# Joined exponentials over a double PSUM tile, and a unit's outputs copied in two halves, in a fused attention and MLP block

## The chip, the cores and the metric

The kernel runs on one core of a Trainium2 chip. The metric is the device time in microseconds (us), the median over runs. The engines of a core are named as the profile names them: PE does matmuls (PEld is its loading of weights), ACT is ScalarE, DVE is VectorE, POOL is GpSimd, and SP issues most of the DMAs. Matmul results land in PSUM, eight banks of 512 fp32 values in each of 128 partitions; ACT and DVE read them from there.

## The reference

All arrays are fp32. One sequence of 2048 tokens with width 512 goes through a layer norm; the result feeds a self-attention with 32 heads of width 16 and an MLP whose output is a gate.

```
def _A_ref(x, wqkv, wo):
    qkv = (x @ wqkv).reshape(B, S, 3, H, Dh) -> q, k, v        # H = 32, Dh = 16
    scores = einsum("bhqd,bhkd->bhqk", q, k) * (Dh ** -0.5)
    p = softmax(scores, axis=-1)
    o = einsum("bhqk,bhkd->bhqd", p, v)
    return o.reshape(B, S, D) @ wo
def _B_ref(x, w1, b1, w2, b2):
    return gelu(x @ w1 + b1) @ w2 + b2                          # 512 -> 1376 -> 512
xn = layernorm(x)
return x + _A_ref(xn, ...) * silu(_B_ref(xn, ...))
```

## The kernel before

The kernel has two parts. The first computes the layer norm, the projections and the MLP, with every product split in high and low parts for precision. The second is the attention. It also ends with the output projection.

**Units and steps.** Heads are taken in 8 groups of 4, queries in 4 chunks of 512. One group and one chunk make a *unit*, so there are 32 units. A unit has 16 *steps*, one for each block of 128 keys, 512 steps in all. In step n (unit `ua`, block `ka` = n mod 16) PE computes for each of the four heads the transposed scores of the block, 128 keys by 512 queries, into one PSUM bank (a *T*, function `t_one`). ACT takes the exponential of each (`slot<-pst` or `slot<-ps` in the profile). PE then multiplies the exponentials of the step *before* with the values, for four heads into one bank `pv` (a *V*, `pv_step`), which sums over the unit's 16 steps. The value matrix carries a column of ones, so that row 16 of each head's 32 output rows is the softmax denominator.

**Maxima.** Before a unit can be exponentiated, the maximum of every row of its scores is needed. This is a second pass over the scores with queries as rows: matmuls of 128 queries by 512 keys (line 183), each followed by a maximum on DVE (line 189). There are 2048 of them. The first part places 576 between its own matmuls (`fill`); the steps of the attention place three each, until they are used up after about 491 steps. In a step two of the three are whole (*S*); the third is made of two halves, *X* and *Y*, of 256 columns each, which share a bank and are reduced together once Y is there. The banks of these matmuls go round in a ring of three (`s_ring`). When a unit's 64 maxima are there, `s_end0` reduces them on DVE (line 242), transposes them (line 246, once for two units as long as the unit is below `PAIRED`), POOL splits them in high and low parts, and `s_send` writes them to DRAM some steps later (`later`, `tick`, `flush`); `load_mh` reads them back as two extra rows of the unit's queries, so that T subtracts them. `need` is the step at which that load is placed.

**Row halves.** T and S use 50 and 48 rows of the array, either the lower 64 rows (`a` = 0) or the upper (`a` = 1). Two matmuls on different halves run side by side. In the first part the matmuls of the projections stand in pairs, one on each half, and `fill(a)` puts a maximum's matmul on one half at a time.

**The order of a step** is written by hand as a string: `ORDER[3]`, with other strings for `ka` 0 and 2 (`AFTER`), and `ORDER[0]` for the last steps, which have no maxima left. There the output projection of the first tokens (`w_halves`) runs instead. `todo` hangs loads, moves and divisions on single T of a step.

**PSUM for T.** Four banks go round: `ps_m` for the first T of a step, the three of `ps_t` for the others.

**End of a unit.** After the sixteenth V, DVE copies the 128 by 512 outputs to the SBUF tile `os` (line 779); only for the last unit ACT copies one half and DVE the other (lines 781, 782). `o_move` sends the denominators and the four heads' rows out of `os` by five DMAs; `o_den` takes reciprocals and spreads them through DRAM (`den_d`, `dn`); `o_div` divides on POOL. `os` is one buffer, and `pv` one bank, so the next unit's first V waits for the copy.

Of the kernel before, what the change touches and what calls it, by code (L numbers as in the profile page):

```python
# [8 lines left out]
F32 = mybir.dt.float32  # L9
# [31 lines left out]
ORDER = {0: "TTTTV", 3: "TSXTTSTYV"}  # L41
AFTER = {0: "STXTTSTYV", 2: "XTSTTYSTV"}
HC = CH // 2
PAIRED = 28
# [6 lines left out]
def fused(ctx: ExitStack, tc: tile.TileContext, x, wqk, wv, wo, w1, b1, w2, b2, out):  # L51
# [7 lines left out]
    ps_t = ctx.enter_context(tc.tile_pool(name="ps_t", bufs=3, space=PSUM))  # L59
    ps_v = ctx.enter_context(tc.tile_pool(name="ps_v", bufs=1, space=PSUM))  # L60
    ps_m = ctx.enter_context(tc.tile_pool(name="ps_m", bufs=1, space=PSUM))

# [4 lines left out]
    den_d = dpool.tile([NG * NCH, GH, CH], F32, name="den_d")  # L67
# [98 lines left out]
    def flush():  # L166
        while later and later[0][0] <= 0:
            u = later.pop(0)[1]
            run_off()
            s_send(u)  # L170
# [36 lines left out]
    def s_op(op):  # L207
# [6 lines left out]
        elif op == "X":  # L214
# [5 lines left out]
            run_off()  # L220
# [11 lines left out]
    def run_off():  # L232
        while put_off:
            put_off.pop(0)()

    def s_end0(u):
# [6 lines left out]
        if u == us[-1]:  # L243
            later.append([12 if "seen" in prog else 8, us[0]])
            nt = qring.tile([P, 2 * GH * NCH], F32, name="nt")
            nc.vector.transpose(nt, nm)
            mh = MH[us[0]] = qring.tile([P, 2, 2 * GH * NCH], F32R, name="mh")

        def two():
            if u == us[-1]:  # L250
                nc.gpsimd.tensor_copy(mh[:, 0], nt)
                nc.gpsimd.tensor_sub(mh[:, 1], nt, mh[:, 0].bitcast(F32))

        put_off.append(two)
        if "seen" in prog or u == NU - 1:
            run_off()
# [128 lines left out]
    with ExitStack() as s1:  # L385
# [4 lines left out]
        def a_tile(shape):  # L390
# [4 lines left out]
            return ps_t.tile(list(shape), F32, name="pst")  # L395
# [220 lines left out]
    def down(c, f, part):  # L616
        i = c * FT + f
        if f == 0 and part == 0:
            PA[c] = [ps_v.tile([P, D], F32, name="pv")] + [ps_t.tile([P, D], F32, name="pst") for t in range(3)]
# [49 lines left out]
    def quad(n, at):  # L669
        us = first[n]  # L670
        for u, b in zip(us, BANKS[n]) if at == 0 else ():
            pool, name = {"x": (ps_x, "ps"), "m": (ps_m, "ps"), "v": (ps_v, "pv"), "t": (ps_t, "pst")}[b]
# [16 lines left out]
    turns, PN = [0], []  # L689

    def t_tile():
        turns[0] += 1
        if turns[0] < 5:
            pool = (ps_m, ps_x, ps_a, ps_b)[turns[0] - 1]
        else:
            pool = ps_m if turns[0] % 4 == 1 else ps_t
        return pool.tile([P, CH], F32, name="pst" if pool is ps_t else "ps")

    def t_one(u, k, p, a):
# [4 lines left out]
        ps = t_tile()  # L704
# [341 lines left out]
```

## Time and profile before

| what | us |
|---|---|
| median of 3 runs | 1563.26 (1563.18 to 1563.92) |
| profiled execution, its own time | 1564.16 |
| span of the profiled execution | 1562.4 |
| PE busy | 1555.6 |
| DVE busy | 1414.8 |
| ACT busy | 1232.5 |
| POOL busy | 366.8 |

All views are of that one execution. The attention takes about the last 1090 us of the span. Three engines are nearly full there, so busy shares alone do not tell which of them sets the pace: one has to look at which wait ends last within a step. A matmul's length in the rows is modelled; its start is not. A row with `x3` is three instructions that followed each other, with the time from the first one's start to the last one's end. Instructions overlap: an exponential's row is 0.60 us long, but the next one starts 0.48 us after it.

### The profile page before, as it was taken

The page shows a single profiled execution, that of the slowest core. Times are in us where ns is not written, and L with a number is a line of the kernel's source. Part 1 is how long each engine was busy: PE and PEld are TensorE (multiplying, and loading weights), DVE is VectorE, ACT ScalarE, POOL GpSimd, SP SyncE. Part 2 cuts the span into 40 slices and gives each one's busy share as a digit, 9 for nine tenths or more (in the row PEclk, how much of TensorE's full clock was granted, in tenths as well). Part 3 has the DMA queues.
Part 4 walks back from the last instruction along what each step waited for, and adds up shares of the span by engine and source line. Part 5 has one row for each costly group of instructions (what it writes and reads, how often), then busy time and mean ns, then how long its engine had stood idle before and what let it go on. Part 6 is the DMA issues. An engine that isn't in the chain of part 4 may idle for free.

```text
span 1562.4 us, 31826 instructions
## 1 busy us (share of the span) xinstructions
PE 1555.6 (100%) x12246; PEld 955.1 (61%) x12246; DVE 1414.8 (91%) x2294; ACT 1232.5 (79%) x2393; POOL 366.8 (23%) x367
## 2 busy tenths in 40 slices
PE   9999999999999999999999999999999999999999
PEld 8899999999994444444444444444444444444455
DVE  7599999999989999999999999999999999999834
ACT  4333332434349999999999999999999999999984
POOL 4145675756650011001000100100010000000143
PEclk9999999999999999999999999999999999999999
DMA  6625343454322123114201411411151111110163
GB/s 209 153 60 152 122 139 100 156 146 136 116 97 62 38 43 59 29 39 63 67 25 27 70 43 30 70 33 29 28 79 26 33 29 33 40 30 22 46 198 114
DMA packets 78584, 116.88 MB, mean 75 GB/s; under 512 B 27972, under 2 KB 28228, under 8 KB 77256
## 3 DMA queue, kind: packets, MB, share of 16 engines
q1 hardware_dynamic: 74684, 101.89, 23.6%
q0 software_dynamic: 3264, 12.35, 4.7%
q8 instruction: 97, 1.59, 0.4%
q14 instruction: 55, 0.45, 0.1%
q10 hardware_dynamic: 484, 0.60, 0.1%
HBM read 84.35 MB, written 25.97 MB: 71 GB/s over the span
## 4 chain that ended last, share of the span: by engine, by line
PE 97%; DVE 1%; DMA 1%; ACT 0%; issue 0%; DVEq 0%
PE pv L772 33%; PE pst L706 14%; PE ps L580 13%; PE ps L706 12%; PE ps L183 12%; PE pst L580 7%; PE pv L580 2%; PE ps L896 1%; PE ps L452 1%; PE ps L81 1%; PE pst L81 0%; DVE st L411 0%; DMA dn<-den_d 0%; DMA xt<-in_x 0%; PE pst L434 0%; DMA dr<-os 0%
## 5 line engine op out<-in xcount | busy, mean ns | idle before, releaser
L189 DVE TENSOR_REDUCE mx<-ps 128x2 f32<-128x512 f32 x2048 | 1316.2, 686 | 83.7 <-PE ps L183 43.1
L708 ACT ACTIVATE slot<-pst 128x512 f32<-128x512 f32 x1533 | 803.9, 606 | 0.6 <-PE ps L706 0.6
L772 PE MATMUL pv<-slot,vsb 128*32 128x512 f32 x4096 | 545.3, 605 | 0.5 <-DVE os L779 0.5
L183 PE MATMUL ps<-kt,slot 48*128 48x512 f32 (+1 forms) x1364 | 378.3, 368 | 0.0
L708 ACT ACTIVATE slot<-ps 128x512 f32<-128x512 f32 x515 | 307.5, 598 | 13.7 <-PE ps L706 6.2
L706 PE MATMUL pst<-qt,kt 50*128 50x512 f32 x1149 | 307.0, 403 | 0.4 <-DVE gt L639 0.3
L183 PEld LDWEIGHTS ps<-kt,slot 48*128 48x128 f32 x1364 | 225.6, 184 | 41.9 <-DVE mx L189 37.3
L706 PEld LDWEIGHTS ps<-qt,kt 50*128 50x128 f32 x387 | 70.6, 183 | 282.7 <-ACT slot L708 281.7
L580 PE MATMUL ps<-slot,w1h 64*128 64x512 f32 x1088 | 226.0, 392 | 0.0
L706 PEld LDWEIGHTS pst<-qt,kt 50*128 50x128 f32 x1149 | 208.1, 185 | 19.3 <-DVE gt L639 1.0
L183 PE MATMUL ps<-kt,qz 48*128 48x512 f32 x512 | 202.6, 396 | 0.0
L706 PE MATMUL ps<-qt,kt 50*128 50x512 f32 x387 | 190.8, 495 | 0.0
L183 PE MATMUL ps<-slot,slot 48*128 48x512 f32 (+1 forms) x598 | 165.8, 367 | 0.0
L580 PEld LDWEIGHTS ps<-slot,w1h 64*128 64x128 f32 x1088 | 155.8, 185 | 7.9
L580 PE MATMUL ps<-slot,w1l 64*128 64x512 f32 x544 | 159.5, 392 | 0.0
L772 PEld LDWEIGHTS pv<-slot,vsb 128*32 128x32 f32 x4096 | 80.7, 108 | 100.0 <-issue 91.1
L364 ACT ACTIVATE hg<-ps,b_sb 128x512 f32<-128x512 f32 x44 | 27.9, 685 | 134.0 <-PE ps L580 122.6
L371 POOL TENSOR_TENSOR hl<-hg,hh 128x512 fp32r<-128x512 f32 x76 | 96.8, 1296 | 153.2 <-ACT hh L370 119.7
L183 PEld LDWEIGHTS ps<-slot,slot 48*128 48x128 f32 x598 | 98.6, 184 | 17.0 <-DVE mx L189 15.3
L706 PE MATMUL pst<-qt,slot 50*128 50x512 f32 x384 | 100.5, 404 | 0.0
L183 PEld LDWEIGHTS ps<-kt,qz 48*128 48x128 f32 x512 | 93.7, 183 | 0.8 <-DVE mx L189 0.5
L810 POOL TENSOR_TENSOR ot<-ot,dn 64x512 f32<-64x512 f32 x15 | 19.2, 1280 | 301.1 <-DMA dn<-den_d 257.6
(159 smaller groups left out, 1718.0 us busy)
## 6 DMA issues: line engine op xcount, KB each, us to landing
raw<-in_w SPq DMA_DIRECT2D x88, 256.0 KB
qk_h<-hh SPq DMA_DIRECT2D x32, 256.0 KB
qk_l<-hl SPq DMA_DIRECT2D x32, 256.0 KB
qt<-qk_h SPq DMA_DIRECT2D x128, 64.0 KB
slot<-qk_h SPq DMA_DIRECT2D x92, 64.0 KB
g_d<-gt POOLq DMA_DIRECT2D x16, 256.0 KB, 3.5
qt<-qk_l SPq DMA_DIRECT2D x64, 64.0 KB
dn<-den_d SPq DMA_DIRECT2D x32, 128.0 KB
```

The lines of the kernel that those rows point to most:

```text
L81: nc.tensor.matmul(ps, lhs[a], rhs[b], start=first and n == 0, stop=last and n == 2)
L183: return nc.tensor.matmul(ps[:, c0:c0 + w], QS[u][r, p, qi * P:(qi + 1) * P], kts[u // NCH % KB][p][r, k0:k0 + w], start=True, stop=True).ins
L189: nc.vector.tensor_reduce(MX[u][:, 2 * p:2 * p + 2, qi, ki][:, heads, parts], ps.rearrange("p (n c) -> p n c", c=HC), axis=AX.X, op=OP.max)
L364: nc.scalar.activation(raw, ph.pop(u), AF.Gelu_apprx_tanh, bias=b1_sb[:, u[2]:u[2] + 1])
L371: nc.gpsimd.tensor_sub(hl, raw, hh.bitcast(F32))
L452: nc.tensor.matmul(pq["q", g, c], W1[g][i][:, k * P:(k + 1) * P], (xh, xl)[j][c][:, k], start=n == 0 and k == 0, stop=n == 2 and k == KT - 1)
L580: i = nc.tensor.matmul(ps, lhs[r], rhs[r], start=first, stop=last).ins
L706: nc.tensor.matmul(ps, kts[g % KB][p][r, k * P:(k + 1) * P], QT[u][r, p, :], start=True, stop=True)
L708: nc.scalar.activation(PT[u, k][:, 2 * p + a, :], ps, AF.Exp, scale=SCALE)
L772: nc.tensor.matmul(PV[u][32 * j:32 * j + 32, :], vsb[:, k, h:h + 32], PT[u, k][:, j, :], start=(k == 0), stop=(k == NT - 1))
L810: eng.tensor_mul(ot[c][rs, g // 2], ot[c][rs, g // 2], DN.pop(u)[rs])
L896: HALF[0] = nc.tensor.matmul(PW[i][0], OTS[i, k][x][r], (wo_h, wo_l)[y][r, k], start=k == 0 and side == 0 and n == 0, stop=k == KT - 1 and ...
```

## The change

- The PSUM pool `ps_t` (three banks) becomes `spare` in the first part, and is closed at the first attention step. In its place come a pool of one bank (`ps_t`) and a tile `two` of two banks, made once.
- `SIDES` gives the four T of a step as (pair of heads, row half). The first goes to `ps_t`, the second and third to the two banks of `two`, the fourth to `ps_m`. The two in `two` are heads 0 and 1 of the group, one on each row half; one exponential of 1024 elements takes both. So a step has three exponentials.
- All steps with three maxima have the order `XTSTTYSTV`; `AFTER` is gone.
- Every unit's outputs are copied by ACT (first 256 columns) and DVE (the others) into two tiles. `o_move` takes 10 DMAs, `o_den` spreads the denominators with 2 instead of 1, and `den_d` has the halves as a dimension.
- `s_end0` leaves the transpose and POOL's two operations to `s_turn`, which runs a step later; in the step with `ka` = 1 neither is done. The sending comes 12 ticks later instead of 8, `need` grows by one or two steps, and `PAIRED` is 26 instead of 28.

```
-ORDER = {0: "TTTTV", 3: "TSXTTSTYV"}
-AFTER = {0: "STXTTSTYV", 2: "XTSTTYSTV"}
+ORDER = {0: "TTTTV", 3: "XTSTTYSTV"}
+SIDES = ((1, 1), (0, 0), (0, 1), (1, 0))
-PAIRED = 28
+PAIRED = 26
...
+    def s_turn(u, nm):
+        later.append([8 if u == NU - 1 else 12, u])
+        nt = qring.tile([P, 2 * GH * NCH], F32, name="nt")
+        nc.vector.transpose(nt, nm)
+        mh = MH[u] = qring.tile([P, 2, 2 * GH * NCH], F32R, name="mh")
+        nc.gpsimd.tensor_copy(mh[:, 0], nt)
+        nc.gpsimd.tensor_sub(mh[:, 1], nt, mh[:, 0].bitcast(F32))
...
+    def t_bank(i):
+        return TP["one"].tile([P, CH], F32, name="pst") if i == 0 else TP["two"][:, i - 1]
+    def t_one(u, k, i, pair=False):
+        p, a = SIDES[i]
...
+        if u == k == 0:
+            ps = (ps_m, ps_x, ps_a, ps_b)[i].tile([P, CH], F32, name="ps")
+        elif i == 3:
+            ps = ps_m.tile([P, CH], F32, name="ps")
+        else:
+            ps = t_bank(i)
...
-        nc.scalar.activation(PT[u, k][:, 2 * p + a, :], ps, AF.Exp, scale=SCALE)
+        if not pair or i in (0, 3):
+            nc.scalar.activation(PT[u, k][:, 2 * p + a, :], ps, AF.Exp, scale=SCALE)
+        elif i == 2:
+            nc.scalar.activation(PT[u, k][:, :2], TP["two"], AF.Exp, scale=SCALE)
...
+    sp.close()
+    TP["one"] = ctx.enter_context(tc.tile_pool(name="ps_t", bufs=1, space=PSUM))
+    TP["two"] = ctx.enter_context(tc.tile_pool(name="ps_2", bufs=1, space=PSUM)).tile([P, 2, CH], F32, name="two")
...
-            OS[u] = wb.tile([P, CH], F32, name="os", bufs=1)
+            OS[u] = [wb.tile([P, HC], F32, name=f"os{i}", bufs=1) for i in range(2)]
             pv = PV.pop(u)
-            if u < NU - 1:
-                nc.vector.tensor_copy(OS[u], pv)
-            else:
-                nc.scalar.activation(OS[u][:, :HC], pv[:, :HC], AF.Copy)
-                nc.vector.tensor_copy(OS[u][:, HC:], pv[:, HC:])
+            nc.scalar.activation(OS[u][0], pv[:, :HC], AF.Copy)
+            nc.vector.tensor_copy(OS[u][1], pv[:, HC:])
...
+        for i in range(2):
+            engs[i].dma_start(DR[u][64 * i:64 * i + 64], os[i][DH::32])
...
-            need = min(n for n in range(L) if due(n) >= 64 * (units_of(u)[-1] + 1)) + (9 if u < PAIRED else 4 if u < NU - 1 else 2)
+            last = units_of(u)[-1]
+            need = min(n for n in range(L) if due(n) >= 64 * (last + 1))
+            need += 10 if u < PAIRED else 6 if u < NU - 1 else 2
...
+        if ka == 1:
+            pass
+        elif put_off:
+            s_turn(*put_off.pop(0))
+        else:
+            for u in list(ended):
+                if u >= PAIRED or ka > 2 and since.setdefault(u, n) < n:
+                    s_end0(u)
```

The order of the instructions shows three places. First PE in an inner step, before (T is L706, S and the 256-column X and Y are L183, V is L772; `kt` are keys, `qt` and `slot_4443` queries, the other slots exponentials):

```order
L706 MATMUL ps<-qt_614,kt_609 128x512
L183 MATMUL ps<-kt_609,slot_4443 128x512
L183 MATMUL ps<-kt_609,slot_4443 128x256
L706 MATMUL pst<-qt_614,kt_609 128x512 x2
L183 MATMUL ps<-kt_609,slot_4443 128x512
L706 MATMUL pst<-qt_614,kt_609 128x512
L183 MATMUL ps<-kt_609,slot_4443 128x256
L772 MATMUL pv<-slot_18503,vsb 32x512 x4
```

and now (T is L703, V is L775):

```order
L183 MATMUL ps<-kt_609,slot_4443 128x256
L703 MATMUL pst<-qt_6826,kt_609 128x512
L183 MATMUL ps<-kt_110,slot_4443 128x512
L703 MATMUL two<-qt_6826,kt_609 128x512 x2
L183 MATMUL ps<-kt_609,slot_4443 128x256
L183 MATMUL ps<-kt_110,slot_4443 128x512
L703 MATMUL ps<-qt_6826,kt_609 128x512
L775 MATMUL pv<-slot_17979,vsb 32x512 x4
```

X has moved to the front, ahead of the first T and the first S; the second S stands behind Y, and the last T is the step's last matmul before V. The second T of the pair follows the first in the program, on the other row half.

Second, ACT in the attention, before, where a change of units leaves no mark on it (a `slot` takes the four exponentials of one step):

```order
L708 ACTIVATE slot_12819<-ps 128x512 [waits PE_49]
L708 ACTIVATE slot_12819<-pst 128x512 [waits PE_49] x3
L708 ACTIVATE slot_12849<-ps 128x512 [waits PE_49]
L708 ACTIVATE slot_12849<-pst 128x512 [waits PE_49] x3
L708 ACTIVATE slot_12883<-ps 128x512 [waits PE_49]
```

and now, over a change of units:

```order
L706 ACTIVATE slot_7218<-pst 128x512
L708 ACTIVATE slot_7218<-two 128x1024
L706 ACTIVATE slot_7218<-ps 128x512
L781 ACTIVATE os_7241<-pv 128x256
L706 ACTIVATE slot_7247<-pst 128x512
L708 ACTIVATE slot_7247<-two 128x1024
L706 ACTIVATE slot_7247<-ps 128x512
```

The half copy stands between the last exponential of one step and the first of the next, and two exponentials have become one of 1024.

Third, DVE from a change of units to the end of a unit's maxima, before (L189 are the maxima, three a step; in brackets the engines and queues whose counters are waited for):

```order
L189 TENSOR_REDUCE mx<-ps 128x2 [waits PE_49] x24
L779 COPY os<-pv 128x512 [waits DMAHW4_49,DMAHW5_49,DMAHW3_49,DMAHW6_49,DVE_49,PE_49]
L189 TENSOR_REDUCE mx<-ps 128x2 [waits PE_49] x9
L242 TENSOR_REDUCE nm_611<-mx 128x16 [waits DVE_49]
L246 STREAM_TRANSPOSE nt<-nm_611 128x32 [waits DVE_49]
L189 TENSOR_REDUCE mx<-ps 128x2 [waits PE_49] x15
```

and now:

```order
L189 TENSOR_REDUCE mx<-ps 128x2 [waits PE_49] x24
L782 COPY os_8564<-pv 128x256 [waits DMAHW3_49,DMAHW5_49,DMAHW1_49,DMAHW7_49,DVE_49,Activation_49]
L189 TENSOR_REDUCE mx<-ps 128x2 [waits PE_49] x9
L245 TENSOR_REDUCE nm_611<-mx 128x16 [waits DVE_49]
L189 TENSOR_REDUCE mx<-ps 128x2 [waits PE_49] x3
L234 STREAM_TRANSPOSE nt<-nm_611 128x32 [waits DVE_49]
L189 TENSOR_REDUCE mx<-ps 128x2 [waits PE_49] x12
```

The copy waits for ACT's counter in place of PE's, and three maxima stand between the reduction and the transpose.

More of the change, by code (lines that the diff above doesn't have):

```diff
@@ L243, in s_end0 @@
         if u == us[-1]:
[L244 to L256, printed above, removed]
+            if "seen" in prog or u == NU - 1:
+                s_turn(us[0], nm)
+            else:
+                put_off.append((us[0], nm))
         del QS[u]
@@ L618, in down @@
         if f == 0 and part == 0:
-            PA[c] = [ps_v.tile([P, D], F32, name="pv")] + [ps_t.tile([P, D], F32, name="pst") for t in range(3)]
+            PA[c] = [ps_v.tile([P, D], F32, name="pv")] + [spare.tile([P, D], F32, name="sp") for t in range(3)]
         h, w = HS[c, f], W2[c, f]
```

61 lines of the change are left out of this document (23 added, 38 removed).

## The prediction

> **What bounds the kernel now.** I read the page first, for the busy shares and the chain of waits, then the table of two stretches, then one attention step instruction by instruction.
>
> ```profile
> PE 1555.6 (100%) x12246; PEld 955.1 (61%) x12246; DVE 1414.8 (91%) x2294; ACT 1232.5 (79%) x2393; POOL 366.8 (23%) x367
> ...
> PE 97%; DVE 1%; DMA 1%; ACT 0%; issue 0%; DVEq 0%
> ```
>
> The kernel seems to belong to PE: busy in all of the span, and 97% of the chain. But a busy PE says little, since the ends of matmuls are modelled. The table of stretches (PE, weight loads, DVE, ACT, POOL, each with its count) shows a second engine as full in the attention part:
>
> ```profile
> 100.00:400.00 300.00, 300.00 (x2568) 284.52 (x2566) 291.58 (x438) 110.37 (x201) 191.13 (x164) 1.00 0.46 134
> 700.00:900.00 200.00, 200.00 (x1560) 93.73 (x1553) 188.62 (x311) 198.59 (x390) 23.09 (x34) 1.00 0.28 50
> ```
>
> From 700 to 900 us ACT is busy 198.6 of 200 us and DVE 188.6. At four exponentials a step, 390 of them are 97.5 steps, so a step takes 2.051 us on average, the stops at unit changes included. Two steps of it (row, start, length; T is line 706, S line 183 with 512 columns, X and Y its halves with 256, V line 772):
>
> ```profile
> 900.30 0.18 PEld L706 LDWEIGHTS ps<-qt,kt 50*128 50x128 f32 x1 [0.84 <-ACT slot L708]
> ...
> 900.31 0.50 PE L183 MATMUL ps<-kt,slot 48*128 48x512 f32 x1
> ...
> 900.64 0.39 PE L706 MATMUL pst<-qt,kt 50*128 50x512 f32 x1
> 900.65 0.28 PE L183 MATMUL ps<-kt,slot 48*128 48x256 f32 x1
> ...
> 900.76 0.39 PE L706 MATMUL pst<-qt,kt 50*128 50x512 f32 x1
> ...
> 900.87 3.90 DVE L189 TENSOR_REDUCE mx<-ps 128x2 f32<-128x512 f32 x6 [0.16 <-PE ps L183]
> 900.87 0.40 PE L183 MATMUL ps<-kt,slot 48*128 48x512 f32 x1
> ...
> 901.11 0.27 PE L183 MATMUL ps<-kt,slot 48*128 48x256 f32 x1
> ...
> 901.32 1.06 PE L772 MATMUL pv<-slot,vsb 128*32 128x512 f32 x8
> 901.33 1.57 ACT L708 ACTIVATE slot<-pst 128x512 f32<-128x512 f32 x3
> ...
> 902.31 0.18 PEld L706 LDWEIGHTS ps<-qt,kt 50*128 50x128 f32 x1 [0.84 <-ACT slot L708]
> ...
> 902.81 0.18 PEld L183 LDWEIGHTS ps<-kt,slot 48*128 48x128 f32 x1
> 902.85 0.60 ACT L708 ACTIVATE slot<-ps 128x512 f32<-128x512 f32 x1
> ...
> 902.95 0.18 PEld L706 LDWEIGHTS pst<-qt,kt 50*128 50x128 f32 x1
> ...
> 903.37 1.06 PE L772 MATMUL pv<-slot,vsb 128*32 128x512 f32 x8
> ...
> 904.37 0.18 PEld L706 LDWEIGHTS ps<-qt,kt 50*128 50x128 f32 x1 [0.84 <-ACT slot L708]
> ...
> 904.93 1.29 DVE L189 TENSOR_REDUCE mx<-ps 128x2 f32<-128x512 f32 x2 [0.16 <-PE ps L183]
> ```
>
> and DVE's work in the attention part by groups:
>
> ```profile
> L189 DVE TENSOR_REDUCE mx<-ps 128x2 f32<-128x512 f32 x1472 | 925.1, 684 | 57.3 <-PE ps L183 27.6 <-PE ps L706 4.3 <-PE pst L706 0.5
> L779 DVE COPY os<-pv 128x512 f32<-128x512 f32 x31 | 21.1, 681 | 0.0
> L242 DVE TENSOR_REDUCE nm<-mx 128x16 f32<-128x128 f32 x24 | 6.7, 278 | 0.1
> L246 DVE STREAM_TRANSPOSE nt<-nm 128x32 f32<-128x32 f32 x14 | 3.0, 212 | 1.3
> ```
>
> The first step takes 900.30 to 902.31 = 2.01 us, the second to 904.37 = 2.06: 4.07 for two, 2.035 each. What makes every second one longer stands in the rows. ACT's first exponential starts 0.54 after its T (902.85 after 902.31); a step's other three, 1.57 together from 901.33, end at 902.90. The bank of the last is what the next step's last T needs: its weights load at 902.95, 0.05 later, V starts 0.42 after that (903.37), the next step 1.00 later (904.37). So ACT closes a loop of two steps of exactly 4.07. DVE closes another: S at 900.31, three reductions from 900.87, 0.68 long and 0.61 apart (two in 1.29 at 904.93), so the third ends at 902.77; the weights of the second S, at 902.81, waited for it. From there a fill of 0.10 (900.30 to 900.64 less the columns), 0.235 for 512 columns (900.64 to 900.87) and 0.21 from Y to V (901.11 to 901.32) end at 903.36. The two loops lie 0.01 to 0.02 apart, and PE's own floor is the fast step, 2.01. ACT is the bound by a hair; a gain on it alone ends at DVE after about 0.02 in two steps.
>
> **The change part by part.**
>
> The last unit of before has its outputs copied in halves already, which gives a size of 256 on each engine (ns: least, median, most):
>
> ```profile
> L781 ACT ACTIVATE os<-pv x1: 386/386/386, 1541.1 to 1541.1; 128x256 f32<-128x256 f32 x1
> ...
> L782 DVE COPY os<-pv x1: 425/425/425, 1541.5 to 1541.5; 128x256 f32<-128x256 f32 x1
> ...
>   ACT os L781: 1.0, 1
> ```
>
> *Joined exponentials.* Two of 512 become one of 1024. The trace has no 1024, but it has 256 and 512 of this engine: 0.386 and 0.60 (902.85), so 0.21 per 256 elements, and 0.43 more than a 512. The last exponential then starts 0.48 + 0.43 = 0.91 after the joined one began, where two apart needed 0.96 (901.33 to the third's start, 1.57 - 0.60 = 0.97). Bounds: 0.86 if the fixed part vanished altogether, 0.97 if nothing did; I take 0.91, since the two sizes give it. ACT's loop falls from 4.07 to about 4.01. Its bank pair is used once a step, and the joined exponential ends about 2.05 after the step's start, before the next step's T there wants weights (0.23 into it): no new wait.
>
> *New order of the step* (X, T, S, T, T, Y, S, T in all steps). DVE's loop: S stands behind the 256 columns of X on its row half, 0.11 to 0.12 later (900.65 to 900.76), so the three reductions shift by that. The last S now ends the step: from it 0.235 + 0.09 to V, in place of 0.235 + 0.21, which returns 0.12. DVE's loop stays at 4.05 to 4.06, and it becomes the bound: 2.0275 a step. PE's columns per row half are the same, 512 three times and 256, so its floor of 2.01 stays, if the two T of the bank pair may start as soon as their own half is free (the rival below). Inner steps: 2048 reductions less 576 made before are 491 steps with three, less 2 at each of 31 unit changes, about 430. 430 x (2.0275 - 2.035) = -3.2 us. Ends: -10.8 if only PE's floor is left (2.01); +3 if the spread of these rows, 0.03 in two steps, falls to the wrong side.
>
> *Outputs in two halves.* The last unit of before has this split already, all others a single DVE copy (rows above). The halves do not run side by side: the DVE half waited 1.0 us until ACT's had ended. In the changed program each DVE half waits for ACT's counter, and ACT's half stands behind the step's last exponential. A unit change of before:
>
> ```profile
> 895.03 1.07 PE L772 MATMUL pv<-slot,vsb 128*32 128x512 f32 x8
> 895.08 1.57 ACT L708 ACTIVATE slot<-pst 128x512 f32<-128x512 f32 x3
> ...
> 896.35 0.68 DVE L779 COPY os<-pv 128x512 f32<-128x512 f32 x1
> ...
> 896.95 3.16 DVE L189 TENSOR_REDUCE mx<-ps 128x2 f32<-128x512 f32 x5
> ...
> 897.12 1.06 PE L772 MATMUL pv<-slot,vsb 128*32 128x512 f32 x8
> ...
> 899.31 0.64 PE L772 MATMUL pv<-slot,vsb 128*32 128x512 f32 x4
> ```
>
> V of the unit's last step runs from 895.03, DVE copies at 896.35 when its own reductions are through, the new unit's V starts at 897.12 and the next at 899.31: 4.28 for two, 0.21 over 4.07. Now with the halves, on the same times: the last exponential starts at 895.08 + 0.91 = 895.99, ACT's half 0.48 later at 896.47 and ends at 896.86 (V's columns ended at 896.10, so ACT's queue decides). DVE's half runs from 896.91 to 897.33, in place of 896.35 to 897.03. V of the new unit can start at 897.38, 0.26 later. Behind the waiting copy on DVE's queue stand the three reductions of the new unit's first step: from 897.25 in place of 896.95. The weights of the last S in the step after wait for the third of them: 897.25 + 2 x 0.61 + 0.68 + 0.04 = 899.19, and 0.42 later V at 899.61, in place of 899.31. So a change costs 0.3 more; I take 0.27, as PE alone would have V at 897.38 + 1.00 + 1.02 = 899.40, earlier, and so hides none of it, but rows spread by 0.03. On ACT the half delays the next first exponential by about 0.1, which its new slack of 0.06 a step takes back in two. 30 changes count (the last lies among the twenty slow steps): +8.1 us. Ends: 0.1 (3 us), if ACT's half slips in ahead of DVE's last reduction; 0.5 (15 us), if both V wait in full.
>
> *End of a unit's maxima.* Before, the 0.28 reduction and the 0.21 transpose stand one behind the other in one step; now the transpose comes a step later, never in the step of the new unit's V:
>
> ```profile
> 691.27 3.73 DVE L189 TENSOR_REDUCE mx<-ps 128x2 f32<-128x512 f32 x6
> ...
> 691.46 1.06 PE L772 MATMUL pv<-slot,vsb 128*32 128x512 f32 x8
> ...
> 693.71 1.07 PE L772 MATMUL pv<-slot,vsb 128*32 128x512 f32 x8
> ```
>
> The reductions of that step began 0.27 late (691.27; a step starts 1.02 before its V, its reductions 0.56 later, at 691.00), and the next step took 691.46 to 693.71 = 2.25, 0.21 over. DVE sits idle 0.16 before each step's first reduction; apart, each piece exceeds that by at most 0.1. Of 14 pairs I count 14 x 0.16 = -2.2 us (ends 0 and -4). POOL's two small operations, the four DMAs of the maxima and the load of their rows come one or two steps later. At the tightest unit (30) the load stands 4 steps, 8 us, ahead of its first T. A mistake there would cost the landing of one DMA, not one per step.
>
> *DMAs.* A unit's move is 10 issues in place of 5, and the denominators' spread 2 in place of 1, all on SP, at 0.59 each:
>
> ```profile
> 899.55 0.59 SPq L795 DMA_DIRECT2D slot<-os  x1
> ```
>
> 3.5 us more of SP's time in the 16 x 2.051 = 33 us of a unit. Behind them stand the query rows of the unit after next, 16 steps ahead: hidden. If not, T would wait for a 0.6 us issue or two. At the very end nothing hides it:
>
> ```profile
> 1542.00 2.84 DMA dr<-os
> ...
> 1546.56 4.51 DMA dn<-den_d
> ```
>
> Two landings instead of one on that chain, and two more issues on ACT's queue ahead of its rounding: +0.5 (0 to +1.5), the pools made at the first attention step included, whose banks wait for the same additions as before.
>
> **Sum.** -3.2 + 8.1 - 2.2 + 0.5 = +3.2 us. The profiled execution took 1564.16 (span 1562.4), 0.9 above the median of the runs; added to the median of 1563.26 it gives 1566.5.
>
> [...]The first window above holds 2568 matmuls in 300 us, two every 0.234 us, the spacing of one row half, though line 183's extra ones are put on one half at a time; were starts kept in program order over both halves, each would have held the other half up. So by this row a matmul passes one that waits for the other half. [...]
>
> **Rivals.**
> *Strict order between the row halves.* The pair's second T, and all behind it on its half, start 0.115 later, V with them: PE's floor is 2.01 + 0.115 = 2.125, +0.09 on 430 steps = +38.7, with the other terms (8.1 - 2.2 + 0.5) 1608.4. For it: nothing in the rows but the order of two instructions; against it the 2568. Chance 0.08.
> *The copies in series cost their upper end, and the steps do not get faster* (the rows' spread on the wrong side): +12 + 3 - 2.2 + 0.5 = +13.3, 1576.6. For it: V waited already 31 times for the copy of before. It decides from 0.4 a change on. Chance 0.15.
> *Faster: PE's floor is reached.* If ACT's loop alone made the long steps and DVE's three reductions settle into the shorter period, steps take 2.01: -10.8 + 8.1 - 2.2 + 0.5 = -4.4, 1558.9, and with unit changes at 0.1 instead of 0.27, 1553.8. It needs a DVE loop of 4.02 or less, 0.03 below what I add up. Chance 0.22.
>
> **How the numbers follow.** A measurement of this kernel tells about 0.2%, 3.1 us, from no change: 1560.1 to 1566.4 is the same. My forecast, 0.55, centres on 1566.5, half of it on either side of the upper edge: 0.26 slower, 0.27 same, 0.02 faster. The rivals add 0.23 slower and 0.22 faster. Faster 0.24, same 0.27, slower 0.49. The range takes the faster rival's middle and the slower one's end, 1555 to 1579, and leaves out the strict order, 0.08, and some 0.1 at both ends.
>
> **What will show it.** Right: the last exponential no longer releases the last T, the pairs of steps last 4.05, the last S waits for DVE; at a unit change the DVE half waits for ACT's and two V intervals last 4.5 to 4.6. Wrong: steps of 2.12 (strict order), of 2.01 (the floor), or unit changes at 4.3. Most of the error would come from the loops: 0.01 a step is 4.3 us.

## The result, and the profile after

| | before | changed |
|---|---|---|
| median of 20 runs each, us | 1563.35 (1563.06 to 1564.34) | 1565.88 (1562.78 to 1568.65) |
| ratio | 1 | 1.0014, 95% interval 1.0008 to 1.0020 |
| profiled execution, us (span) | 1564.16 (1562.4) | 1564.97 (1563.0) |
| first V starts | 469.39 | 470.80 |
| first to second V | 2.60 | 3.78 |
| 2nd to 479th V | 980.6 | 976.8 |
| an inner step, mean | 2.0365 (398 steps) | 2.0165 (415) |
| two V intervals at a unit change, mean of 29 | 4.253 | 4.532 |
| steps of 2.1 or more among the rest, and their excess | 21, 3.9 us | 4, 0.5 us |
| 479th to 511th V | 86.6 | 87.5 |
| 511th V to the end of the span | 23.3 | 24.1 |

The lower rows are differences of the starts of V (line 772 before, 775 now), counted through the attention part. There are 512 V; the last follows 0.9 behind the 511th, with no step between them, so the count ends with the 511th. So a change of 0.14% is the sum of five differences of 2 to 8 us with both signs (start, inner steps, unit changes, long steps, end), and the runs of the changed kernel lie 5.9 us apart where those of before lie 1.3 apart.

The page of the changed kernel: busy times, the chain that ended last, and two groups.

```profile
PE 1547.5 (99%) x12246; PEld 921.3 (59%) x12246; DVE 1407.6 (90%) x2295; ACT 1219.6 (78%) x1913; POOL 367.4 (24%) x369
...
PE 59%; ACT 35%; issue 2%; DVE 2%; DMA 1%; SPq 1%; ACTq 0%; POOL 0%; POOLq 0%; DVEq 0%
...
L708 ACT ACTIVATE slot<-two 128x1024 f32<-128x1024 f32 x511 | 521.5, 1021 | 4.0 <-PE ps L703 3.0
...
L703 PEld LDWEIGHTS two<-qt,kt 50*128 50x128 f32 x766 | 115.1, 186 | 1.0 <-ACT slot L708 0.3
```

The joined exponential takes 1.021, as the two sizes of before gave (0.60 + 0.43), and the T that write its bank pair waited 1.0 us in 766: the double tile is free in time. ACT's 35% of the chain mean little; the stretch of 200 us and three inner steps say more:

```profile
700.00:900.00 200.00, 198.42 (x1564) 88.06 (x1557) 187.40 (x312) 196.48 (x300) 23.07 (x34) 1.00 0.27 50
```

```profile
901.79 0.18 PEld L183 LDWEIGHTS ps<-kt,slot 48*128 48x128 f32 x1 [0.84 <-DVE mx L189]
...
902.01 0.39 PE L183 MATMUL ps<-kt,slot 48*128 48x512 f32 x1
...
902.13 0.50 PE L703 MATMUL two<-qt,kt 50*128 50x512 f32 x2
...
902.24 0.18 PEld L703 LDWEIGHTS ps<-qt,kt 50*128 50x128 f32 x1
...
902.43 3.92 DVE L189 TENSOR_REDUCE mx<-ps 128x2 f32<-128x512 f32 x6 [0.25 <-PE ps L183]
...
902.81 1.06 PE L775 MATMUL pv<-slot,vsb 128*32 128x512 f32 x8
...
904.82 1.06 PE L775 MATMUL pv<-slot,vsb 128*32 128x512 f32 x8
```

V at 900.79, 902.81, 904.82, 906.83: every step takes 2.01 to 2.02, none 2.06. The weights of the last T (902.24) wait for nothing any more. The 0.84 beside the weights of X (901.79), which opens the step now, is not VectorE's doing: each step has it, before the change too (0.84 at 902.31, where the label named ACT), it is the time in which V holds TensorE, and the label only names the semaphore that came last. TensorE's own work is what is left. The second row of T's also answers the strict order: S at 902.01 has 512 columns on one row half, where before 0.235 lay between two starts (900.64 and 900.87), and a T of the pair starts 0.12 later. By these spacings I take it for the pair's second, on the other half, and the T at 902.24 (902.13 + 0.50 - 0.39, the length of one) for the first, written ahead of it, 0.23 behind S; the rows themselves do not name the half.

A unit change of the changed kernel (V of the unit's last step at 896.25):

```profile
896.25 1.07 PE L775 MATMUL pv<-slot,vsb 128*32 128x512 f32 x8
...
897.17 0.60 ACT L706 ACTIVATE slot<-ps 128x512 f32<-128x512 f32 x1
...
897.65 0.40 ACT L781 ACTIVATE os<-pv 128x256 f32<-128x256 f32 x1
...
898.09 0.42 DVE L782 COPY os<-pv 128x256 f32<-128x256 f32 x1 [0.30 <-ACT os L781]
...
898.57 1.06 PE L775 MATMUL pv<-slot,vsb 128*32 128x512 f32 x8 [0.23 <-DVE os L782]
...
900.79 1.06 PE L775 MATMUL pv<-slot,vsb 128*32 128x512 f32 x8
```

ACT's half starts 0.48 after its last exponential, DVE's half waits for it, V for that: 2.32 and 2.22.

What I had not looked for stands at the first attention step. Three lines of the timeline, and two-microsecond stretches (the column 1.00 or 0.50 is the granted clock):

```profile
467.73 0.39 PE L574 MATMUL sp<-w2h,hl 64*128 64x512 f32 x1
467.91 1.87 DVE L633 TENSOR_TENSOR gt<-sp,b_sb 128x512 f32<-128x512 f32 x3
...
469.84 0.50 PE L703 MATMUL pst<-qt,kt 50*128 50x512 f32 x1 [1.72 <-DVE gt L633]
```

```profile
468.00:470.00 2.00, 0.28 (x3) 0.16 (x4) 1.79 (x3) 1.17 (x3) 1.61 (x3) 1.00 1.07 338
470.00:472.00 2.00, 2.00 (x13) 0.52 (x13) 1.29 (x2) 1.51 (x2) 0.56 (x2) 0.65 0.98 334
472.00:474.00 2.00, 2.00 (x11) 1.25 (x8) 0.00 (x0) 0.51 (x2) 0.00 (x0) 0.50 0.42 164
474.00:476.00 2.00, 2.00 (x17) 0.89 (x16) 1.87 (x3) 1.99 (x4) 0.00 (x0) 1.00 0.03 8
```

Before, each T took a bank as soon as VectorE's addition had left it, with a wait of 0.28:

```profile
468.36 0.49 PE L706 MATMUL pst<-qt,kt 50*128 50x512 f32 x1 [0.28 <-DVE gt L639]
```

Now the pool of three banks is closed as a whole, and the first T waits for the last of the additions: TensorE stands still for 1.72. Then the clock falls to 0.50, from about 470.6 to 474.0 (0.35 x 2.00 / 0.50 = 1.4 us in the second stretch, 2.0 in the third: 3.4), and V takes 1.93 in place of 1.06.

### The profile page after: what moved, and what is told of

Same layout as the page of the kernel before. It is cut to its first block, busy times and chain, and to the rows that moved or that the text cites. A ratio compares the mean times of both kernels' runs of the same rounds, so it can differ in the third digit from the quotient of the medians.

```text
span 1563.0 us, 31698 instructions
## 1 busy us (share of the span) xinstructions
PE 1547.5 (99%) x12246; PEld 921.3 (59%) x12246; DVE 1407.6 (90%) x2295; ACT 1219.6 (78%) x1913; POOL 367.4 (24%) x369
## 4 chain that ended last, share of the span: by engine, by line
PE 59%; ACT 35%; issue 2%; DVE 2%; DMA 1%; SPq 1%; ACTq 0%; POOL 0%; POOLq 0%; DVEq 0%
ACT slot L706 20%; ACT slot L708 15%; PE pv L775 14%; PE ps L574 13%; PE ps L183 12%; PE sp L574 7%; PE two L703 3%; PE pv L574 2%; PE pst L703 2%; PE ps L703 1%; PE ps L899 1%; PE ps L82 1%; PE ps L446 1%; DVE os L782 1%; ACT os L781 1%
## 5 line engine op out<-in xcount | busy, mean ns | idle before, releaser
L189 DVE TENSOR_REDUCE mx<-ps 128x2 f32<-128x512 f32 x2048 | 1316.4, 686 | 81.1 <-PE ps L183 29.4
L775 PE MATMUL pv<-slot,vsb 128*32 128x512 f32 x4096 | 546.2, 605 | 7.3 <-DVE os L782 7.3
L708 ACT ACTIVATE slot<-two 128x1024 f32<-128x1024 f32 x511 | 521.5, 1021 | 4.0 <-PE ps L703 3.0
L183 PEld LDWEIGHTS ps<-kt,slot 48*128 48x128 f32 x1364 | 214.7, 184 | 298.3 <-DVE mx L189 288.9
L183 PE MATMUL ps<-kt,slot 48*128 48x256 f32 (+1 forms) x1364 | 376.2, 365 | 0.0
L706 ACT ACTIVATE slot<-pst 128x512 f32<-128x512 f32 x511 | 306.5, 600 | 20.5 <-PE pst L703 9.3
L706 ACT ACTIVATE slot<-ps 128x512 f32<-128x512 f32 x515 | 312.0, 606 | 1.6 <-PE pst L703 1.6
L703 PE MATMUL two<-qt,kt 50*128 50x512 f32 x766 | 205.6, 397 | 0.0
L183 PE MATMUL ps<-kt,qz 48*128 48x512 f32 x512 | 202.2, 395 | 0.0
L703 PE MATMUL pst<-qt,kt 50*128 50x512 f32 x383 | 190.2, 497 | 1.7 <-DVE gt L633 1.7
L183 PEld LDWEIGHTS ps<-slot,slot 48*128 48x128 f32 x598 | 94.6, 185 | 130.6 <-DVE mx L189 126.3
L183 PE MATMUL ps<-slot,slot 48*128 48x256 f32 (+1 forms) x598 | 164.5, 365 | 0.0
L775 PEld LDWEIGHTS pv<-slot,vsb 128*32 128x32 f32 x4096 | 80.8, 108 | 140.0 <-issue 122.4
L703 PE MATMUL ps<-qt,kt 50*128 50x512 f32 x387 | 155.1, 402 | 0.0
L703 PEld LDWEIGHTS two<-qt,kt 50*128 50x128 f32 x766 | 115.1, 186 | 1.0 <-ACT slot L708 0.3
L183 PEld LDWEIGHTS ps<-kt,qz 48*128 48x128 f32 x512 | 93.7, 183 | 1.0 <-DVE mx L189 0.7
```

The source lines that it names most:

```text
L183: return nc.tensor.matmul(ps[:, c0:c0 + w], QS[u][r, p, qi * P:(qi + 1) * P], kts[u // NCH % KB][p][r, k0:k0 + w], start=True, stop=True).ins
L189: nc.vector.tensor_reduce(MX[u][:, 2 * p:2 * p + 2, qi, ki][:, heads, parts], ps.rearrange("p (n c) -> p n c", c=HC), axis=AX.X, op=OP.max)
L703: nc.tensor.matmul(ps, kts[g % KB][p][r, k * P:(k + 1) * P], QT[u][r, p, :], start=True, stop=True)
L706: nc.scalar.activation(PT[u, k][:, 2 * p + a, :], ps, AF.Exp, scale=SCALE)
L708: nc.scalar.activation(PT[u, k][:, :2], TP["two"], AF.Exp, scale=SCALE)
L775: nc.tensor.matmul(PV[u][32 * j:32 * j + 32, :], vsb[:, k, h:h + 32], PT[u, k][:, j, :], start=(k == 0), stop=(k == NT - 1))
```

## The experiments

All are read against the changed kernel (1565.88) or the kernel before (1563.51 to 1563.59 in each comparison, so that they can be set side by side), by median, and by the same counts of V starts as above.

**One copy.** The halves undone; DMAs stay in halves.

```diff
-OS[u] = [wb.tile([P, HC], F32, name=f"os{i}", bufs=1) for i in range(2)]
+os = wb.tile([P, CH], F32, name="os", bufs=1)
+OS[u] = [os[:, :HC], os[:, HC:]]
...
-nc.scalar.activation(OS[u][0], pv[:, :HC], AF.Copy)
-nc.vector.tensor_copy(OS[u][1], pv[:, HC:])
+nc.vector.tensor_copy(os, pv)      # the last unit: halves as before
```

> The changed kernel with one part undone: a unit's outputs are copied by VectorE alone into one tile, as before (the last unit excepted); the DMAs stay cut in halves. Theory: the ScalarE half and the VectorE half run one after the other and hold the new unit's V and VectorE's reductions; two V intervals at a unit change go from 4.53 back to 4.25, 30 of them make -8.4 us, and the time is about 1557.5 against 1565.9 of the changed kernel. Rival: the unit change is longer because of the new order of the step, which puts VectorE's reductions 0.11 later in the step; then it stays at 4.5 and the time within 2 us of 1565.9.

1561.38 (1559.54 to 1564.12), ratio to before 0.9987 (0.9978 to 0.9996). Unit changes take 4.393: neither 4.25 nor 4.53. So leaving out the halves gives back half of the 0.28 (0.14 x 30 = 4.2 us; the medians differ by 4.5), and the other half stays, by something else that the change brings.

**S first at a unit's first step.** That half which stays. Joined exponentials, outputs copied and moved as before, banks given up a step later (the kernel of "both", below), and one order more:

```diff
 ORDER = {0: "TTTTV", 3: "XTSTTYSTV"}
+AFTER = {0: "STXTTSTYV"}
...
+if want == 3 and ua:
+    order = AFTER.get(ka, order)
```

> The kernel with joined exponentials, the outputs copied and moved as before and the banks given up a step later (1557.8), with one order changed: the first step of a unit is S T X T T S T Y V, as in the kernel before, all others X T S T T Y S T V. With the new order its unit changes take 4.39, 0.36 over two steps, in the kernel before 4.25, 0.18 over two steps. Theory: the copy stands behind the three reductions of that step, which the order with X first puts 0.11 later; with S first unit changes fall to 4.25, 30 x 0.14 = -4.2, 1553.6. Rival: the longer unit change comes from the joined exponential, whose bank pair is free later at the step after: within 1 us of 1557.8.

1554.10 (1554.00 to 1554.75) against 1557.77 without that line. The copy of "both", then with S first, and the V next to each:

```profile
892.93 1.06 PE L774 MATMUL pv<-slot,vsb 128*32 128x512 f32 x8
894.35 0.68 DVE L781 COPY os<-pv 128x512 f32<-128x512 f32 x1
895.08 1.06 PE L774 MATMUL pv<-slot,vsb 128*32 128x512 f32 x8
897.30 1.06 PE L774 MATMUL pv<-slot,vsb 128*32 128x512 f32 x8
```

```profile
891.53 1.06 PE L775 MATMUL pv<-slot,vsb 128*32 128x512 f32 x8
892.74 0.68 DVE L782 COPY os<-pv 128x512 f32<-128x512 f32 x1
893.55 1.06 PE L775 MATMUL pv<-slot,vsb 128*32 128x512 f32 x8
895.70 1.06 PE L775 MATMUL pv<-slot,vsb 128*32 128x512 f32 x8
```

The copy starts 1.42 after V, or 1.21; the intervals are 2.15 + 2.22, or 2.02 + 2.15. The two intervals fall by 0.22 (4.391 to 4.174), the step ahead of them grows by 0.10, which leaves 0.12 x 30 = 3.6 of the 3.7 measured. With X ahead, VectorE's three reductions come later and the copy behind them.

**VectorE's half first.**

```diff
-nc.scalar.activation(OS[u][0], pv[:, :HC], AF.Copy)
 nc.vector.tensor_copy(OS[u][1], pv[:, HC:])
+nc.scalar.activation(OS[u][0], pv[:, :HC], AF.Copy)
```

> The changed kernel with VectorE's half of the copy issued ahead of ScalarE's. If what costs is that VectorE's three reductions stand behind a copy which waits for ScalarE: VectorE's half starts 0.28 earlier, unit changes fall from 4.53 to about 4.3, -7, 1559. If the halves exclude each other whatever comes first: ScalarE's half ends at the same time or later, and now holds the next step's exponentials by 0.7: unit changes of 4.6 to 5.2, +2 to +20, 1568 to 1586.

1570.99 (1569.82 to 1571.87); unit changes 4.640. The second of the two holds: the halves exclude each other in either order.

```profile
899.67 0.42 DVE L781 COPY os<-pv 128x256 f32<-128x256 f32 x1
900.12 0.38 ACT L782 ACTIVATE os<-pv 128x256 f32<-128x256 f32 x1 [0.37 <-DVE os L781]
```

**The old order of the step,** joined exponentials kept.

```diff
-ORDER = {0: "TTTTV", 3: "XTSTTYSTV"}
+ORDER = {0: "TTTTV", 3: "TSXTTSTYV"}
+AFTER = {0: "STXTTSTYV", 2: "XTSTTYSTV"}
```

> The changed kernel with the old order of the step (T S X T T S T Y V, and the two other orders at the start of a unit), the joined exponentials kept. Theory of ScalarE's loop alone: the joined exponential is enough, steps stay at 2.0165, within 2 us of 1565.9. My prediction's reading of VectorE's loop (the second S waits for the third reduction, 4.05 in two steps): 2.0275 a step, +4.7, 1570.6. Theory of the order: 2.0365, +8.6, 1574.5.

1571.06 (1568.30 to 1573.32), and steps of 2.0264: the loop of VectorE, 4.053 for two, where the prediction had put it, at 4.05 to 4.06. Unit changes take 4.548 here, 0.295 more than in the kernel before, though the order is the old one: in it the halves cost the whole of what the change costs. So the halves (0.295 alone) and the order (0.14 alone, in "one copy") do not add up; with both it is 0.28.

**No joining,** first with two exponentials on the double tile.

```diff
-if not pair or i in (0, 3):
-    nc.scalar.activation(PT[u, k][:, 2 * p + a, :], ps, AF.Exp, scale=SCALE)
-elif i == 2:
-    nc.scalar.activation(PT[u, k][:, :2], TP["two"], AF.Exp, scale=SCALE)
+nc.scalar.activation(PT[u, k][:, 2 * p + a, :], ps, AF.Exp, scale=SCALE)
```

> The changed kernel, order, banks and double tile kept, but two exponentials of 512 in place of each joined one of 1024. Theory of ScalarE's loop (the short step of 2.01 comes from the joined exponential, which saves ScalarE 0.06 a step): every second step is long again, 2.035 a step on average, +0.019 on about 430 steps, +8, 1574. Rival, the order's theory (the last T now stands later in the step, its bank is free in time even with four exponentials, and VectorE's last reduction is what the order freed): steps stay at 2.0165 and the time within 2 us of 1565.9.

3198.68 us (3195.74 to 3199.78), twice the time, which neither theory has. The double tile is guarded as one: its second T waits for the first one's exponential, and the clock, once it has fallen at 471 us, stays at 0.50 up to 3099 us, 2628 us long (its mean is 0.589 over the span of 3196.6):

```profile
2001.05 0.28 PEld L703 LDWEIGHTS two<-qt,kt 50*128 50x128 f32 x1 [1.41 <-ACT slot L705]
2001.05 0.79 PE L703 MATMUL two<-qt,kt 50*128 50x512 f32 x1 [0.69 <-ACT slot L705]
```

```profile
700.00:900.00 200.00, 173.54 (x596) 64.84 (x595) 76.08 (x120) 89.92 (x153) 9.03 (x16) 0.50 0.09 18
```

A pause of 0.69 in every step of 5.35, and 200 us at a clock of 0.50 though TensorE is busy for 173.5 of them. This told nothing of the exponentials, so the same with two single banks:

```diff
-TP["two"] = ctx.enter_context(tc.tile_pool(name="ps_2", bufs=1, space=PSUM)).tile([P, 2, CH], F32, name="two")
+TP["two"] = ctx.enter_context(tc.tile_pool(name="ps_2", bufs=2, space=PSUM))
```

> The changed kernel with two exponentials of 512 in place of the joined one of 1024, and with the double tile replaced by two single banks, so that each T waits only for its own bank. With the old order and joined exponentials a step took 2.0264, with both changes 2.0165, with neither 2.0365. If both loops have to be shortened and ScalarE's is at 4.07 without the joining: 2.035, +8, 1574. If each change gives its own 0.01: 2.0265, +4.2, 1570. If the order alone does it: 2.0165, within 1.5 us of 1565.9.

1572.12 (1571.62 to 1574.88), steps of 2.038, alternately short and long again (starts of V):

```profile
903.19 1.07 PE L772 MATMUL pv<-slot,vsb 128*32 128x512 f32 x8
905.20 1.06 PE L772 MATMUL pv<-slot,vsb 128*32 128x512 f32 x8
907.26 1.07 PE L772 MATMUL pv<-slot,vsb 128*32 128x512 f32 x8
```

| step, us | old order | new order |
|---|---|---|
| four exponentials | 2.0365 | 2.038 |
| two and a joined one | 2.0264 | 2.0165 |

Two loops, as predicted: the order alone gives nothing, the joining alone 0.010, and the order another 0.010 once ACT's loop is out of the way.

**The transpose at once.**

```diff
-if "seen" in prog or u == NU - 1:
-    s_turn(us[0], nm)
-else:
-    put_off.append((us[0], nm))
+s_turn(us[0], nm)
```

> The changed kernel with the transpose of a pair's maxima issued at once behind their reduction, as before, not a step later. Theory: 0.28 and 0.21 together exceed VectorE's idle 0.16 of a step, each time a step is late by 0.2 to 0.25; 13 or 14 pairs in the attention part: +3 us, 1569. Rival: the outlying steps went with the new order, in which VectorE's reductions have more room, not with the transpose's place: within 1 us of 1565.9.

1570.30 (1566.54 to 1572.80). In the profile, two steps at the lower clock aside, 17 steps of 2.1 or more exceed the others by 4.2 us in all, against 4 steps and 0.5 us: +3.7, as the first theory has it. In the changed kernel the reduction and the transpose of that unit stand in two steps, and both steps stay at 2.02 (V at 691.45, 693.47 and 695.49):

```profile
692.90 0.28 DVE L245 TENSOR_REDUCE nm<-mx 128x16 f32<-128x128 f32 x1
...
694.90 0.20 DVE L234 STREAM_TRANSPOSE nt<-nm 128x32 f32<-128x32 f32 x1
```

**The banks given up a step later.** In step 1 the first T takes the fourth bank, the others the three old single banks; the double tile is made behind step 1.

```diff
-sp.close()                      # ahead of the first attention step
...
-elif i == 3:
+elif u == 0 and k == 1 and i:
+    ps, pair = spare.tile([P, CH], F32, name="sp"), False
+elif i == 3 or u == 0 and k == 1:
     ps = ps_m.tile([P, CH], F32, name="ps")
...
+if n == 1:
+    sp.close()                  # then the pools of "pst" and "two"
```

> The changed kernel, but the three single PSUM banks of the part ahead of attention are given up one attention step later: in attention step 1 the first T takes the bank of the fourth, the other three single banks with an exponential each, and the double tile is made at step 2. Theory: TensorE's pause of 2.1 us at the first attention step, in which it waits for all of VectorE's additions at once, is what lets the granted clock fall to 0.5 for 3.4 us and more; without it the clock stays at 1.00, the first V comes at 469.4 in place of 470.8 and the second 2.6 later in place of 3.8, the runs lie within 1.5 us of each other as those of the kernel before do, and the median is 1562 to 1563.5 (-2.4 to -4). Rival: the lower clock and the wide spread of the runs come from elsewhere (the steps of 2.01, with TensorE more densely loaded, or the last steps); then at most the 1.4 us of the first V come back, and the runs still spread over 5 us.

1563.58 (1562.35 to 1566.31): -2.3. The first V comes at 469.60, the second 3.19 later, the clock is 1.00 throughout. But the runs still lie 4 us apart, so the clock is not the whole of the spread. The two longest, 1566.31 and 1566.02, exceed their own spans by 3.3 and 2.8 us, the others by 1.8 to 2.1; the spans alone lie 2.6 apart.

**The kernel before with the banks given up.**

```diff
-ps_t = ctx.enter_context(tc.tile_pool(name="ps_t", bufs=3, space=PSUM))
+spare = sp.enter_context(tc.tile_pool(name="spare", bufs=3, space=PSUM))
...
+sp.close()                      # ahead of the first attention step
+ps_t = ctx.enter_context(tc.tile_pool(name="ps_t", bufs=3, space=PSUM))
```

> The kernel before with this alone added: the three single PSUM banks of the first part are given up and made again at the first attention step (no double tile). TensorE then waits there for VectorE's last addition. Theory: the first V comes 0.5 to 1.4 later; in part of the runs the clock falls to 0.5 for 3.4 us behind the pause, +1.2 to +3 more, so that the median rises by 1 to 4 us and the runs lie several us apart, where those of the kernel before lie within 1.5. Rival: one T on a free bank breaks the pause (in the kernel before the first T has one), the clock stays at 1.00, and the time rises by 0.4 to 1 us with the runs as close together as before.

1565.47 (1564.23 to 1567.27) against 1563.51, ratio 1.0014 (1.0005 to 1.0023): this edit alone costs 2.0 us, and it spreads the runs over 3.0. One T on a free bank doesn't break the pause; its profile has the wait and then the clock at 0.50:

```profile
467.79 0.40 PE L708 MATMUL ps<-qt,kt 50*128 50x512 f32 x1
469.67 0.51 PE L708 MATMUL pst<-qt,kt 50*128 50x512 f32 x1 [1.48 <-DVE gt L641]
```

```profile
470.00:472.00 2.00, 2.00 (x12) 0.20 (x8) 1.29 (x2) 1.08 (x2) 0.45 (x1) 0.50 1.01 369
```

**Five DMAs a unit.** Halves copied by both engines, into one tile, moved and spread as before.

```diff
+OS[u] = wb.tile([P, CH], F32, name="os", bufs=1)
+nc.scalar.activation(OS[u][:, :HC], pv[:, :HC], AF.Copy)
+nc.vector.tensor_copy(OS[u][:, HC:], pv[:, HC:])
...
+engs[0].dma_start(DR[u], OS[u][DH::32])            # and four "ot", one "dn"
```

> The changed kernel with the halves of the outputs copied by ScalarE and VectorE into one tile, which is moved by five DMAs a unit and spread by one, as before. Theory: the doubled DMAs stand on SP's queue in the last twenty steps, the denominators come late there, the division on GpSimd with them, and TensorE waits for the rounding behind it; at the end SP's four more issues hold the last denominators by 0.9. So the last steps lose their waits of 0.5 to 1 us at the step that waits (87.0 us from the 479th V to the last in place of 87.5 to 88.9), from the last V to the end 23.0 to 23.3 in place of 24.1 to 24.6, in all -1.4 to -3, 1563 to 1564.5, and the runs lie closer together. Unit changes stay at 4.53. Rival, DMAs hidden as I predicted: within 0.7 us of 1565.9.

1564.60 (1562.61 to 1565.97): -1.3, little beside runs that lie 3.4 and 5.9 us apart. The profiles say the same: from the 479th V to the 511th 86.9, from there to the end 23.1, so 0.6 and 1.0 less. The last denominators of the changed kernel, then with five DMAs: from the first issue to the division 10.1 us, or 8.8.

```profile
1541.38 1.14 ACTq L793 DMA_DIRECT2D dr<-os  x1
...
1544.67 0.25 DVE L802 RECIPROCAL dr<-dr 128x16 f32<-128x16 f32 x1 [2.86 <-DMA dr<-os]
...
1551.48 0.69 DVE L813 TENSOR_TENSOR ot<-ot,dn 64x512 f32<-64x512 f32 x1 [1.79 <-DMA dn<-den_d]
```

```profile
1542.18 1.14 ACTq L792 DMA_DIRECT2D dr<-os  x1
1545.15 0.25 DVE L800 RECIPROCAL dr<-dr 128x16 f32<-128x16 f32 x1 [3.00 <-DMA dr<-os]
...
1550.93 0.69 DVE L810 TENSOR_TENSOR ot<-ot,dn 64x512 f32<-64x512 f32 x1 [1.38 <-DMA dn<-den_d]
```

In the last twenty steps the doubled DMAs hold TensorE too, through GpSimd: the division waits for its denominators, the rounding stands behind the division, TensorE's product behind that. The wait differs from profile to profile: 0.24 in the changed kernel, 0.72 with the banks late, none with five DMAs; these rows are of "one copy".

```profile
1508.62 1.28 POOL L817 TENSOR_TENSOR ot<-ot,dn 64x512 f32<-64x512 f32 x1 [6.53 <-DMA dn<-den_d]
1509.98 1.27 POOL L884 TENSOR_TENSOR ol<-slot,oh 128x512 fp32r<-128x512 f32 x1
...
1511.30 0.50 PE L903 MATMUL ps<-wo_h,ol 64*128 64x512 f32 x2 [0.70 <-POOL ol L884]
```

**Both: outputs as before, banks late.** The diffs of "the banks" and the outputs' part of the kernel before; joined exponentials, order and maxima of the changed kernel.

> Joined exponentials, new order of the step and the split end of the maxima of the changed kernel, with the outputs copied and moved as before (one copy, five DMAs a unit) and the banks given up one step later. If the terms add: steps at 2.0165 for 2.0365 (-8.4), unit changes at 4.25 (0), maxima -3.4, first steps 0, tail 0 to -0.8: 1551 to 1553, 0.7% under the kernel before. If unit changes are longer by the new order or the pause returns a step later: 1554 to 1560.

1557.77, five runs from 1557.65 to 1558.34, ratio 0.9962 (0.9950 to 0.9975). The parts add: one copy -4.5, banks -2.3, DMAs -1.3 make -8.1, and 1565.88 - 8.1 is 1557.8; that it fits to 0.1 is in part luck, as runs that lie 3.4 to 5.9 us apart leave about 1 us of doubt in each part. With both sources gone the runs lie 0.7 apart. My 1551 to 1553 took unit changes at 4.25 for granted; they stayed at 4.39 until S came first. With that line the kernel takes 1554.10, ratio 0.9939 (0.9927 to 0.9952): 9.4 us under the kernel before.

## Why the prediction was right, and where it was right by luck

The forecast, 1566.5, lies 0.6 over the median. By the prediction's own line of 1566.4 the result counts as the same, to which it gave a chance of 0.27; the likeliest to it was slower, 0.49. Its terms do not lie as close as the sum:

| term | predicted | measured | by |
|---|---|---|---|
| steps | -3.2 | -8.3 | (2.0165 - 2.0365) x 415 |
| unit changes | +8.1 | +8.4 | (4.532 - 4.253) x 30 |
| maxima | -2.2 | -3.4 | excess of long steps; +3.7 when undone |
| start and end | +0.5 | +4.4 | banks and clock 3.1 (2.3 undone, and 0.8 by which the second V is still later then), DMAs 1.3 |

The measured column adds up to +1.1 where the medians differ by 2.5. Its upper rows come from one profile each, and 1.4 us stay without a row.

*Steps.* Wrong: "DVE's loop stays at 4.05 to 4.06, and it becomes the bound". ACT's half of the working held (the joined exponential 1.021, the last T free of waits), and DVE's loop is at 4.053 with the old order. What failed is the step that the new order returns to it only what it takes. Over 218 inner steps of before and 229 of the changed kernel, VectorE's first reduction starts 0.573 and 0.653 after the step began, a shift of 0.08, not 0.11 to 0.12 (S starts 0.22 later than X, but its reduction follows 0.43 after it, where it took 0.57 with an S that opens the step). And from the S that waits for the third reduction to V it is 0.47 before and 0.33 now, 0.14 back, not 0.12. So the loop falls by 0.06, from 4.053 to 3.99, under the 4.02 of two fast steps. The rival "PE's floor is reached" was the right one for the steps.

*Unit changes.* Right in size, and half right in cause. The rows went as drawn (ACT's half 0.48 after its last exponential, V 2.32 and 2.22 where I had 2.35 and 2.23), and in the old order the halves do cost that much (4.548 against 4.253). But I put all of the 0.27 on them. Had they been left out, the order would still have cost 0.14: X ahead of S in the unit's first step delays the reductions in front of the copy. I counted that shift on the inner steps and forgot it here. With the halves it does not show: VectorE then sits idle for 0.30 in front of its half (898.09), until ACT's has ended.

*Maxima.* Right, 1.2 us too small: "each piece exceeds that by at most 0.1" was the careful end.

*DMAs.* "Hidden" holds for the 29 units in the middle (unit changes of 4.531 with five DMAs, 4.532 with ten) and fails in the last twenty steps, where GpSimd divides and rounds in turn; at the very end the 0.9 is within my 0 to +1.5.

*The start.* The failing step is "the pools made at the first attention step included, whose banks wait for the same additions as before". They wait for the last of them together, not each for its own. The direct price was 1.4; the clock's fall behind it was in no term.

*Strict order* did not happen: an inner step takes 2.0165, not 2.12. The rows at 902.01 and 902.13 speak against it too: 0.12 lies between these starts, where a T that stands behind S on its half would come 0.235 later.

So 5 us more gain in the steps and 4 us more loss at the start and end: a sum right by compensation. Had the start alone been as I drew it, the time would have been near 1563.

## What to carry to other kernels

Where two loops lie within 0.02 of each other, price an edit on both together: either alone returned half or nothing here. An order that is better in the inner step may be worse at a step with another job in it, so keep the exceptions. Closing banks for a new pool at a seam of the program can turn small waits into one large one (here a wait of 0.28 became one of 1.72), and that can cost nearly as much behind it as in itself: in the changed kernel the first V came 1.41 later, and with the clock at 0.50 the second another 1.18.

## What the hardware showed that I had not expected

After the same pause of 1.72 the granted clock differs from one execution to the next. In the profile of "one copy" it stays at 1.00 (second V 2.61 after the first), in that of the changed kernel it is 0.50 for 3.4 us, in that of "five DMAs" for 6.8 (next rows: 0.66 and 0.63 at the ends of it, so 1.36 + 4 + 1.48), where the first two intervals of V are 3.70 and 3.64.

```profile
470.00:472.00 2.00, 2.00 (x13) 0.45 (x12) 1.29 (x2) 1.37 (x2) 0.10 (x1) 0.66 0.95 365
472.00:474.00 2.00, 2.00 (x13) 1.46 (x15) 0.83 (x2) 1.47 (x3) 0.00 (x0) 0.50 0.18 70
474.00:476.00 2.00, 2.00 (x10) 0.34 (x12) 1.06 (x2) 1.12 (x2) 0.00 (x0) 0.50 0.11 32
476.00:478.00 2.00, 2.00 (x12) 1.29 (x16) 1.17 (x2) 1.34 (x2) 0.00 (x0) 0.63 0.56 132
```

Over the changed kernel's 20 runs the mean granted clock and the time go together: those at 1.000 took 1562.8 to 1564.8, those at 0.997 took 1565.9 to 1568.7. With 0.69 in every step the clock stayed at 0.50 for 2628 us with two exponentials on the double tile; that these pauses held it down is not shown.

The lengths of the stretches at one clock have a common measure in two traces. In the changed kernel's, the record of the clock begins at 6.37 with 1.00, changes to 0.50 at 470.58, to 1.00 at 474.00 and to 0.50 at 1562.85; in that of before it begins at 5.60 with 1.00 and changes to 0.50 at 1562.07. The stretch of before lasts 1556.478, the three whole ones of the changed kernel 464.213, 3.413 and 1088.852. That is 456, 136, 1 and 319 times 3.41333 (1556.478 / 456), to within 0.001. In the other profiles the two-microsecond stretches from 468 to 480 agree with one or two times that, within the 0.04 that their rounding leaves: 3.44 at 0.50 in the kernel before with the banks given up, 6.84 with five DMAs, 6.84 with the transpose at once, 6.80 with VectorE's half first.

Counted back by 3.413 from the fall, the pause lies inside one such length in the three profiles whose rows show both: in the changed kernel from 468.13 to 469.84 (467.17 to 470.58), with five DMAs from 467.60 to 469.32 (467.23 to 470.64), in the kernel before with the banks given up from 468.19 to 469.67 (466.59 to 470.00). That the place of the pause decides is not shown by this: a pause of 1.72 lies inside a length of 3.413 by chance half the time (1 - 1.72 / 3.413), and in "one copy", where the clock stayed at 1.00, no row shows where the lengths begin. How long a pause has to be stays open: 1.48 was followed by the fall in the kernel before with the banks given up, and 1.72 was not in "one copy". Why the clock stays down for 3.4 us or for 6.8 stays open too.
